# Five small moves in an attention-then-experts kernel: buffers, weight fetches, decay rows, PSUM banks, token products

## The chip, the cores and the metric

The kernel runs on one core of one Trainium2 chip. The metric is the device time of one execution in microseconds (us), here the median over several runs. The engines are TensorE (PE, with its weight loads shown apart as PEld), VectorE (DVE), ScalarE (ACT), GpSimd (POOL) and SyncE (SP, which only issues DMAs here). All data is float32, but for the one-hot rows of the token lists, which are float16.

## The reference

```python
# attention: q, k, v, alpha are (B=4, H=8, S=768, D=48); alpha lies in 0.8 to 1.0
for t in range(S):
    state = alpha[:, :, t, :, None] * state + einsum('bhd,bhe->bhde', k[:, :, t], v[:, :, t])
    y[:, :, t] = einsum('bhd,bhde->bhe', q[:, :, t], state)

# experts: x is y with its heads side by side, (N=3072, Dm=384); E=8 experts, F=1024
logits = x @ w_gate
expert = argmax(logits, axis=1)
gate_w = softmax(logits) at expert
out[n] = gate_w[n] * (relu(x[n] @ w1[expert[n]]) @ w2[expert[n]])
```

Each token goes to one expert only, and every token is kept, whatever the load of its expert.

## The kernel before

**Order.** The program is written under a manual schedule: each engine executes its instructions in the order in which the Python code emits them, and waits by semaphores for what an instruction needs. There is no planner. So a call that moves in the code moves on every engine, and a DMA stands in the queue of the engine that issues it: loads, row copies and weights on SP, the decay rows on ACT, gathers and scatters on POOL. The DMAs of SP and ACT share eight semaphores in a ring, so each of them also waits for the one eight issues earlier.

**Attention.** The sequence is cut into 6 chunks of 128 time steps. With 4 batches this makes 24 tiles; tile `s` is chunk `s // 4` of batch `s % 4`. The loop `for i in range(-4, NT)` runs one step per tile (about 5.45 us in the middle) and works on several tiles at once:

- `loads_for` fetches q, k, v and alpha, mostly for two tiles together (384 KB a load), some steps ahead.
- `logs` (L387) takes ln of alpha on ACT into `lna`; `cums` sums it over time on PE (L392, tile `cum`) and takes `icp` = exp(-sum) and `cp` = exp(sum) on ACT (L395, L396).
- `decay_out` copies the first row of `icp` of a tile, for the tile's own chunk, and the last row of `cp`, for the next chunk, into a small tile `dec` with one DMA each on the ACT queue (L408). With a chunk's first batch it also loads one row of alpha, `alpha0`, on SP (L411).
- `decay_rows` (L416, L417, POOL) multiplies these to `er`, the decay from one chunk to the next; `decay_cols` turns `er` on PE (`ep`, L428) and copies it to `E` (L430). `scale_state` (L475, POOL) makes `U`, the state times `E`.
- `operands` (L437, POOL) makes `kqb`, k times `icp` and q times `cp`, for tile `i + 2`; `transposes` (L447) turns it, with DVE copying `qT` (L451) and ACT `kT` (L453) out of PSUM.
- `scores` (L460, `sA` and `sB`), `mask` (L468, `dA` and `dB`), `read_state` (L487, reads `U`), `attend` (L497) and `keys_values` (L508) make the output of a tile in PSUM (`y`); ACT copies it to `yT` (L516). `rows` (L534) turns it into token rows `x`, and with them come the logits.
- `logits`, `gate` (L548, `gex`) and `gate_weight` choose the expert and its weight; `keep_rows` writes the weighted token row from `x` to `xs` (L559, ACT) and copies it to `x_rows` in DRAM by a DMA of 192 KB on SP (L560). The tile `xs` has the pool's default of two buffers.
- `fetch_part` fetches expert 0's weights in ten pieces (six of w1 with 256 KB, four of w2 with 384 KB), one per step from i=4 to i=13. `late_consts` makes constants of the routing on POOL, in five portions at i=1 to i=5.

In the first steps (i = -4 to 2) more than one tile is summed per step: `new_sums(i)` gives two tiles at i=1 and i=2 (tiles 4, 5 and 6, 7, chunk 1), and one afterwards.

**Between the two halves.** Expert 0's first 256 tokens are gathered before attention has ended. `early_layer1(f)` (L626) computes the block f of 8 of their hidden layer. `tokens` (L298) multiplies the one-hot rows of the last 8 tiles into the token lists `tok`; `place_experts` (L306 to L324) orders the experts by load; `weights(1, 1)` fetches the next expert's weights on SP; `decode` (L333 to L347) reads `tok` and gives in its first four operations (`ag`, `au`, `agi`) the indices of the gathers, and after that those of the scatters.

**Experts.** The experts are worked off in eight places, the largest group first after expert 0. Place 0 is the rest of expert 0's tokens (168 rows): `gather`, `early_layer2` (L1083, the second layer of the early 256 tokens), `rest_layer1` (L1095, 8 blocks into PSUM banks, the relus in turn on ACT, L1103, and DVE, L1100, with pieces of the DVE work `beside` in between) and `rest_layer2` (L1111, three blocks `d`, copied to `zT` at L1114). Places 1 to 7 use a scheme with seven products instead of eight (L875, L933, L948). PSUM has the tags `tp`, `pA`, `pB` and `pC` with two banks each. `scatter` copies a block of rows out of PSUM (`zo`, L965, ACT) and writes it to the tokens' places in `out` with an indirect DMA on POOL (L966); the rows of the last place come from `rows_layer2` (L992).

Of the kernel before, what the change touches and what calls it, by code (L numbers as in the profile page):

```python
# [8 lines left out]
F32 = mybir.dt.float32  # L9
# [9 lines left out]
def kernel(  # L19
# [343 lines left out]
    with tc.tile_pool(name="ld", bufs=6) as ld, \  # L363
# [32 lines left out]
            nc.scalar.activation(cp[:], cum[:, :Dm], AF.Exp)  # L396
            st[s]["cp"], st[s]["icp"] = cp, icp

        def decay_out(s):
            c, b = cb(s)  # L400
            cp, icp = st[s]["cp"], st[s]["icp"]


            for cc, i, row in ((c, 1, icp[0:1, :]), (c + 1, 0, cp[C - 1 :, :])):
                if 0 < cc < NB:
                    if cc not in decay:
                        decay[cc] = work.tile([B, 2, Dm], F32, name="dec", bufs=3)
                    nc.scalar.dma_start(decay[cc][b : b + 1, i, :], row)  # L408
            if b == 0 and c + 1 < NB:
                alpha0[c + 1] = work.tile([B, H, D], F32, name="alpha0", bufs=3)  # L410
                nc.sync.dma_start(alpha0[c + 1][:], alpha[:, :, (c + 1) * C, :])  # L411

# [142 lines left out]
        def keep_rows(s):  # L555

            d = st[s]
            xs = work.tile([C, NP, D2], F32, name="xs")
            nc.scalar.activation(xs[:], d["x"][:, :, :D2], AF.Copy, scale=d["gw"][:])  # L559
            nc.sync.dma_start(x_d[s * C : (s + 1) * C, :], xs[:].rearrange("p m d -> p (m d)"))  # L560
            st[s] = {n: t_ for n, t_ in d.items() if n == "acc"}
# [106 lines left out]
        for i in range(-4, NT):  # L668
            loads_for(i)
            do(scores, i)  # L670
            if i < NT - 1:
                do(result, i - 1)
            do(logits, i - 2)
            if i >= B:
                do(add_state, i - 1)
            do(gate, i - 2)
            if i > 0:
                for s in new_sums(i):
                    logs(s)
            if i == NT - 1:  # L680
                early_turn()
            if 0 < i < NT and i % B == 0:
                decay_cols(i // B)
            do(mask, i, 0)
            do(mask, i, 1)
            if i < B:
                do(add_state, i - 1)
            do(transposes, i + 1)
            sums = list(new_sums(i))
            for s in sums[:1]:  # L690
                cums(s)
            if i < 0:
                for s in sums[1:]:
                    cums(s, "x")
            do(gate_weight, i - 2)
            route(i)
            do(keep_rows, i - 2)
            if i < 0 or len(sums) == 1:
                for s in sums:
                    decay_out(s)  # L700
            if i == NT - 2:
                si = next(se)[1]
                eg["si"] = lambda j, r: si[:r, j : j + 1]
            do(operands, i + 2)
            if i % B == 0:
                do(scale_state, i)
            if 0 < i + 1 < NT and (i + 1) % B == 0:
                decay_rows((i + 1) // B)
            elif i >= 0:
                do(scale_state, i + 1)  # L710
            one_hots(nc.gpsimd, *on_gpsimd.get(i, ()))
            do(read_state, i)
            do(attend, i)
            if i == NT - 2:
                result(i)
            if i >= 0 and sums[1:]:
                cums(sums[1])
                for s in sums:
                    decay_out(s)
            do(keys_values, i)  # L720
            if i == NT - 3:
                held["tok"] = ps.tile([C, NC], F32, name="tok", tag="cum")
                tokens(held["tok"][:], *range((NG - 1) * TG))
                se = early_gather()
            do(rows, i - 1)
            if i in counts_in:
                counts(counts_in[i], counted(i - 1))
            if i < 0:
                for s in new_sums(i + 1):
                    logs(s)  # L730
            if i == -3:
                second_consts()
            late_consts(i - 1)
            if 4 <= i < 14:
                fetch_part(groups[0], i - 4)


        last = NT - 1
# [16 lines left out]
        keep_rows(last)  # L755
        slots(NG - 1, cps)
        rows_cols(NG - 1)
        for f in range(3, FB):
            early_layer1(f)
        for s in range((NG - 1) * TG, NT):  # L760
            one_hots(nc.vector, s)
            tokens(held["tok"][:], s)
        place_experts()
        weights(1, 1)
        d = decode(held["tok"][:], NC, "a")
        g_e = next(d)
        _, s_e, gf_e, sf_e = next(d)


# [190 lines left out]

        return p1, rest

    def scatter(g, j, r, zp):
        zo = wk.tile([C, Dm], F32, name="zo", bufs=3)
        nc.scalar.copy(zo[:r], zp)  # L965
        ins = nc.gpsimd.indirect_dma_start(  # L966
            out=out[:, :], out_offset=bass.IndirectOffsetOnAxis(ap=g["si"](j, r), axis=0),
            in_=zo[:r], in_offset=None, bounds_check=N - 1, oob_is_err=False,
# [119 lines left out]
    def rest_layer1(g, beside):  # L1088
        n = g["n"]
        g["h"] = wk.tile([C, FB, CAP0], F32, name="h_sb")  # L1090
        for f in range(FB):
            t = "pB" if f % 2 else "pC"
            hp = mps.tile([C, 512], F32, name=t, tag=t)
            for a in range(DB):
                nc.tensor.matmul(  # L1095
# [44 lines left out]
    for i, g in enumerate(groups):  # L1140
# [39 lines left out]
        if last:  # L1180
            for j, r in blocks(g):
                rows_layer2(g, j, (*([] if j == 0 else ready), FH - 1, FB - 1))
                scatter(g, j, r, g["z"][:r, :Dm])
        elif i:
            rest[0](lambda: ahead(*((1,) if i == E - 2 else (1, 2))), between)
        else:
# [59 lines left out]
```

## Time and profile before

| | |
|---|---|
| runs, us | 432.89, 425.61, 425.33, 430.03, 426.73, 426.06 |
| median, us | 426.4 |
| profiled execution, us | 426.63 |
| its span (first to last instruction), us | 424.8 |
| mean granted clock of TensorE | 0.993 |
| PE busy, us | 405.5 (95% of the span) |
| DVE, ACT, POOL busy, us | 207.8, 171.1, 143.8 |
| DMA moved | 59.08 MB, 139 GB/s on average |

The span is from the first to the last instruction of the profiled execution; the execution's own time is 1.8 us longer. Times of instructions are counted from the start of the span. In a row of the timeline the first number is the start, the second the duration, then come engine, line, operation, tiles and shapes; a bracket at the end gives the idle time of the engine before the row, and what ended it. "SPq" and "ACTq" rows are a queue issuing DMAs. A granted clock of 1.00 is full speed, and 0.50 is half.

### The profile page before, as it was taken

To read this page: it belongs to the slowest core of one execution; us is meant where nothing else is said; L and a number is where in the kernel's file an instruction comes from. 1 tells how busy PE (TensorE), PEld (TensorE's weight loads), DVE (VectorE), ACT (ScalarE), POOL (GpSimd) and SP (SyncE) were. 2 spreads that over 40 slices of the span, in tenths; PEclk is the share of its full clock that TensorE was granted. 3 is DMA by queue.
4 is the path that set the end of the run, shared out by engine and by line. 5 is a ranking of instruction groups with operands and counts; after the bars stand their busy time and mean duration, and the time that the engine had idled before them with its cause. 6 is when DMAs were issued, how large, how long until landed. Compare 5 with 4: busy or idle time off the path is not lost.

```text
span 424.8 us, 9224 instructions
## 1 busy us (share of the span) xinstructions
PE 405.5 (95%) x3525; PEld 342.1 (81%) x3525; DVE 207.8 (49%) x643; ACT 171.1 (40%) x453; POOL 143.8 (34%) x193
## 2 busy tenths in 40 slices
PE   7988999997999999889999999999999999999995
PEld 4757888886888885789879979979979979979952
DVE  5442555563565665174663563473473483453200
ACT  4564566564665430114413513513523523513510
POOL 3438464678558203602300340240240240200101
PEclk9998999999999999999999999999999999999998
DMA  9999999899851217644235054252351352300101
GB/s 172 189 201 209 224 242 205 210 233 233 184 124 39 96 39 253 225 149 169 75 137 169 37 210 128 78 207 74 132 205 60 144 203 58 145 1 2 51 20 35
DMA packets 120098, 59.08 MB, mean 139 GB/s; under 512 B 102934, under 2 KB 114287, under 8 KB 120052
## 3 DMA queue, kind: packets, MB, share of 16 engines
q1 hardware_dynamic: 114932, 48.80, 43.7%
q0 software_dynamic: 3424, 9.59, 6.4%
q8 instruction: 29, 0.48, 0.5%
q10 hardware_dynamic: 1696, 0.08, 0.3%
q14 instruction: 17, 0.14, 0.1%
HBM read 48.95 MB, written 9.58 MB: 138 GB/s over the span
## 4 chain that ended last, share of the span: by engine, by line
PE 82%; issue 6%; DMA 5%; DVE 3%; ACT 2%; POOL 1%; ACTq 0%; POOLq 0%; SPq 0%
PE pA L875 10%; PE pB L875 8%; PE pC L948 8%; PE pA L933 7%; PE y L497 5%; PE sA L460 5%; PE tp L447 5%; PE pB L933 4%; PE pC L875 4%; PE x L534 4%; PE cum L392 4%; PE y L487 3%; PE pC L933 2%; PE tp L791 2%; PE tp L626 2%
## 5 line engine op out<-in xcount | busy, mean ns | idle before, releaser
L966 POOL DMA_INDIRECT out_dram<-zo,sp x25 | 27.0, 1079 | 169.6 <-ACT zo L965 118.9
L184 DVE TENSOR_TENSOR h_sb<-pB,u 128x208 f32<-128x208 f32 (+6 forms) x56 | 20.1, 359 | 60.9 <-PE pB L875 43.1
L819 ACT COPY u<-pA 128x208 f32<-128x208 f32 (+6 forms) x68 | 21.6, 317 | 54.0 <-PE pA L933 50.3
L437 POOL TENSOR_TENSOR kqb<-k_sb,icp 128x384 f32<-128x384 f32 x23 | 22.9, 998 | 43.9 <-PE y L508 16.6
L948 PE MATMUL pC<-h_sb,w 128*128 128x416 f32 (+5 forms) x96 | 32.9, 496 | 0.0
L875 PE MATMUL pA<-t,s 128*128 128x208 f32 (+6 forms) x112 | 28.6, 337 | 0.6
L460 PE MATMUL sA<-qT,kT 48*128 48x128 f32 x192 | 28.0, 286 | 0.9 <-DVE qT L451 0.9
L781 POOL DMA_INDIRECT xg<-x_rows,gp x25 | 25.9, 1034 | 7.6 <-issue 6.1
L460 PE MATMUL sB<-qT,kT 48*128 48x128 f32 x192 | 28.0, 286 | 0.0
L948 PEld LDWEIGHTS pC<-h_sb,w 128*128 128x128 f32 x96 | 18.1, 190 | 12.0 <-issue 4.4
L875 PE MATMUL pA<-xgT,w 128*128 128x208 f32 (+6 forms) x112 | 27.7, 329 | 0.0
L460 PEld LDWEIGHTS sA<-qT,kT 48*128 48x128 f32 x192 | 23.4, 189 | 3.9 <-ACT kT L453 1.1
L541 DVE TENSOR_REDUCE lgn<-x 128x8 f32<-128x32 f32 x23 | 4.4, 191 | 45.3 <-PE x L534 40.3
L447 PE MATMUL tp<-ident,kqb 128*128 128x128 f32 x192 | 25.9, 278 | 0.6 <-DVE kqb L437 0.6
L534 PE MATMUL x<-iw,yT 128*64 128x104 f32 x368 | 21.6, 261 | 2.4 <-ACT xs L559 2.3
L875 PE MATMUL pB<-t,w 128*128 128x208 f32 (+6 forms) x112 | 23.4, 331 | 0.2 <-DVE h_sb L184 0.2
L447 PEld LDWEIGHTS tp<-ident,kqb 128*128 128x128 f32 x192 | 20.8, 140 | 3.4 <-issue 1.2
L460 PEld LDWEIGHTS sB<-qT,kT 48*128 48x128 f32 x192 | 23.4, 189 | 0.0
L437 POOL TENSOR_TENSOR kqb<-q_sb,cp 128x384 f32<-128x384 f32 x23 | 22.9, 998 | 0.6 <-DMA q_sb<-in_q_dram 0.3
L875 PE MATMUL pC<-xgT,w 128*128 128x208 f32 (+6 forms) x112 | 23.1, 329 | 0.0
L888 ACT ACTIVATE h_sb<-h_sb 128x416 f32<-128x416 f32 (+6 forms) x28 | 14.8, 530 | 20.5 <-DVE h_sb L184 20.1
L468 DVE TENSOR_TENSOR dA<-sA,cmask 128x512 f32<-128x512 f32 x24 | 16.5, 689 | 12.2 <-PE sB L460 12.2
(245 smaller groups left out, 957.0 us busy)
## 6 DMA issues: line engine op xcount, KB each, us to landing
w<-in_moe_w_dram SPq DMA_DIRECT2D x14, 1536.0 KB, 7.2
x_rows<-xs SPq DMA_DIRECT2D x24, 192.0 KB, 3.2
v_sb<-in_v_dram SPq DMA_DIRECT2D x10, 384.0 KB, 6.3
k_sb<-in_k_dram SPq DMA_DIRECT2D x9, 384.0 KB, 6.6
q_sb<-in_q_dram SPq DMA_DIRECT2D x9, 384.0 KB, 5.3
a_sb<-in_alpha_dram SPq DMA_DIRECT2D x8, 384.0 KB, 4.7
a_sb<-in_alpha_dram SPq DMA_DIRECT2D x8, 192.0 KB, 3.9
w<-in_moe_w_dram SPq DMA_DIRECT2D x6, 256.0 KB, 4.3
```

Source lines behind the costliest of these rows:

```text
L184: eng.tensor_tensor(out, a, b, op=ALU.add)
L437: eng.tensor_tensor(by_half(kq[:, i]), d[n].rearrange("s (a p) d -> s a p d", a=2), d[e][:].rearrange("s (a p d) -> s a p d", a=2, p=NP), ...
L447: nc.tensor.transpose(tp[:, p, :], pair(kqb[s % 3][:, i], p), ident[:])
L460: nc.tensor.matmul(t[:, p, :], lhsT=d["kT"][r : r + D, p, :], rhs=d["qT"][r : r + D, p, :], start=True, stop=True,)
L497: nc.tensor.matmul(yv(g)[o : o + D, j, :], lhsT=d["v"][:, g * NP + p, :], rhs=d["d" + "AB"[g]][:, p, :], start=(s < B and j == 0), stop=Tr ...
L534: nc.tensor.matmul(d["x"][o : o + HC, m, : D2 + E], lhsT=d["yT"][:, m // 2, m % 2, o : o + HC], rhs=iw[:, m, :], start=True, stop=True,)
L781: nc.gpsimd.indirect_dma_start(out=g["xg"][:r, j, :], out_offset=None, in_=x_d[:, :], in_offset=bass.IndirectOffsetOnAxis(ap=g["gi"](j, r) ...
L819: nc.scalar.copy(t[:, :m], bank["A"][:, :m])
L875: nc.tensor.matmul(out, lhsT=ops[n_][0], rhs=ops[n_][1], start=first and n_ == names[0], stop=True, skip_group_check=True,)
L933: nc.tensor.matmul(out, lhsT=lhs, rhs=rhs, start=first and f == 0, stop=True, skip_group_check=True)
L948: nc.tensor.matmul(d2[:, :n], lhsT=w2[:, f, 2 * C :], rhs=h[:, f, :n], start=(f == 0), stop=(f == FB - 1),)
L966: ins = nc.gpsimd.indirect_dma_start(out=out[:, :], out_offset=bass.IndirectOffsetOnAxis(ap=g["si"](j, r), axis=0), in_=zo[:r], in_offset= ...
```

## The change

- The tile `xs` gets four buffers instead of two. The ten pieces of expert 0's weights are fetched at i=12 to 21 instead of i=4 to 13.
- `decay_out` takes an argument that says which of its two rows to copy. For chunk 1, steps i=1 and i=2 copy only the `icp` rows, two DMAs instead of four; the `cp` rows of tiles 4 to 7 follow at i=3 to 6, one in each step, next to the two DMAs that these steps have already. `alpha0` of chunk 2 goes with the first of them. The rows of tiles 0 and 1 are copied at i=-1. `late_consts` is called at i=-4 (three portions), 0 and 1.
- `rest_layer1` takes its PSUM banks in turn from `pC`, `pB` and `pA` instead of `pC` and `pB`.
- The last token products come before the last block of `early_layer1` instead of after it, and the first part of `decode` comes before `place_experts`.
- The last scatter's rows (112 of them) are copied half by DVE and half by ACT, out of the same bank.

```diff
--- before.py
+++ after.py
@@ -396,17 +396,18 @@
             nc.scalar.activation(cp[:], cum[:, :Dm], AF.Exp)
             st[s]["cp"], st[s]["icp"] = cp, icp
 
-        def decay_out(s):
+        def decay_out(s, which=(0, 1)):
             c, b = cb(s)
             cp, icp = st[s]["cp"], st[s]["icp"]
 
 
-            for cc, i, row in ((c, 1, icp[0:1, :]), (c + 1, 0, cp[C - 1 :, :])):
+            for j in which:
+                cc, row = ((c, icp[0:1, :]), (c + 1, cp[C - 1 :, :]))[j]
                 if 0 < cc < NB:
                     if cc not in decay:
                         decay[cc] = work.tile([B, 2, Dm], F32, name="dec", bufs=3)
-                    nc.scalar.dma_start(decay[cc][b : b + 1, i, :], row)
-            if b == 0 and c + 1 < NB:
+                    nc.scalar.dma_start(decay[cc][b : b + 1, 1 - j, :], row)
+            if b == 0 and c + 1 < NB and 1 in which:
                 alpha0[c + 1] = work.tile([B, H, D], F32, name="alpha0", bufs=3)
                 nc.sync.dma_start(alpha0[c + 1][:], alpha[:, :, (c + 1) * C, :])
 
@@ -555,7 +556,7 @@
         def keep_rows(s):
 
             d = st[s]
-            xs = work.tile([C, NP, D2], F32, name="xs")
+            xs = work.tile([C, NP, D2], F32, name="xs", bufs=4)
             nc.scalar.activation(xs[:], d["x"][:, :, :D2], AF.Copy, scale=d["gw"][:])
             nc.sync.dma_start(x_d[s * C : (s + 1) * C, :], xs[:].rearrange("p m d -> p (m d)"))
             st[s] = {n: t_ for n, t_ in d.items() if n == "acc"}
@@ -695,9 +696,14 @@
             do(gate_weight, i - 2)
             route(i)
             do(keep_rows, i - 2)
-            if i < 0 or len(sums) == 1:
-                for s in sums:
+            if len(sums) == 1:
+                decay_out(sums[0])
+            if i == -1:
+                for s in range(2):
                     decay_out(s)
+
+            if B - 1 <= i < 2 * B - 1:
+                decay_out(i + 1, (1,))
             if i == NT - 2:
                 si = next(se)[1]
                 eg["si"] = lambda j, r: si[:r, j : j + 1]
@@ -716,7 +722,7 @@
             if i >= 0 and sums[1:]:
                 cums(sums[1])
                 for s in sums:
-                    decay_out(s)
+                    decay_out(s, (0,) if i else (0, 1))
             do(keys_values, i)
             if i == NT - 3:
                 held["tok"] = ps.tile([C, NC], F32, name="tok", tag="cum")
@@ -730,9 +736,11 @@
                     logs(s)
             if i == -3:
                 second_consts()
-            late_consts(i - 1)
-            if 4 <= i < 14:
-                fetch_part(groups[0], i - 4)
+            if i in (-4, 0, 1):
+                for j in {-4: (0, 1, 2), 0: (3,), 1: (4,)}[i]:
+                    late_consts(j)
+            if 12 <= i < 22:
+                fetch_part(groups[0], i - 12)
 
 
         last = NT - 1
@@ -755,15 +763,16 @@
         keep_rows(last)
         slots(NG - 1, cps)
         rows_cols(NG - 1)
-        for f in range(3, FB):
+        for f in range(3, FB - 1):
             early_layer1(f)
         for s in range((NG - 1) * TG, NT):
             one_hots(nc.vector, s)
             tokens(held["tok"][:], s)
+        early_layer1(FB - 1)
+        d = decode(held["tok"][:], NC, "a")
+        g_e = next(d)
         place_experts()
         weights(1, 1)
-        d = decode(held["tok"][:], NC, "a")
-        g_e = next(d)
         _, s_e, gf_e, sf_e = next(d)
 
 
@@ -960,9 +969,13 @@
 
         return p1, rest
 
-    def scatter(g, j, r, zp):
+    def scatter(g, j, r, zp, shared=False):
         zo = wk.tile([C, Dm], F32, name="zo", bufs=3)
-        nc.scalar.copy(zo[:r], zp)
+        if shared:
+            nc.vector.tensor_copy(zo[:r, : Dm // 2], zp[:, : Dm // 2])
+            nc.scalar.copy(zo[:r, Dm // 2 :], zp[:, Dm // 2 :])
+        else:
+            nc.scalar.copy(zo[:r], zp)
         ins = nc.gpsimd.indirect_dma_start(
             out=out[:, :], out_offset=bass.IndirectOffsetOnAxis(ap=g["si"](j, r), axis=0),
             in_=zo[:r], in_offset=None, bounds_check=N - 1, oob_is_err=False,
@@ -1089,7 +1102,7 @@
         n = g["n"]
         g["h"] = wk.tile([C, FB, CAP0], F32, name="h_sb")
         for f in range(FB):
-            t = "pB" if f % 2 else "pC"
+            t = "p" + "CBA"[f % 3]
             hp = mps.tile([C, 512], F32, name=t, tag=t)
             for a in range(DB):
                 nc.tensor.matmul(
@@ -1180,7 +1193,7 @@
         if last:
             for j, r in blocks(g):
                 rows_layer2(g, j, (*([] if j == 0 else ready), FH - 1, FB - 1))
-                scatter(g, j, r, g["z"][:r, :Dm])
+                scatter(g, j, r, g["z"][:r, :Dm], shared=j == NJ - 2)
         elif i:
             rest[0](lambda: ahead(*((1,) if i == E - 2 else (1, 2))), between)
         else:
```

## The prediction

> **What bounds the kernel now.** I read the page first, then PE's gaps in the timeline, then the engine that each gap names.
>
> ```profile
> PE 405.5 (95%) x3525; PEld 342.1 (81%) x3525; DVE 207.8 (49%) x643; ACT 171.1 (40%) x453; POOL 143.8 (34%) x193
> ...
> DMA  9999999899851217644235054252351352300101
> ```
>
> PE is busy 405.5 of 424.8 us, and the change takes no matmul away. So it can win only from PE's 19.3 us of idle, or from PE's clock. The second line says that DMA is full for the first ten slices (106 us) and has room afterwards.
>
> The timeline of PE; the bracket is PE's idle before the row and what ended it:
>
> ```profile
> 23.15 0.91 PE L392 MATMUL cum<-lna,cum_m 128*128 128x384 f32 x2 [0.64 <-ACT lna L387]
> ...
> 30.33 0.91 PE L392 MATMUL cum<-lna,cum_m 128*128 128x384 f32 x2 [1.05 <-ACT lna L387]
> ...
> 38.58 0.66 PE L487 MATMUL y<-qT,U 48*48 48x128 f32 x16 [1.71 <-POOL U L475]
> ...
> 105.83 0.93 PE L534 MATMUL x<-iw,yT 128*64 128x104 f32 x16 [2.33 <-ACT xs L559]
> ...
> 160.86 7.98 PE L1083 MATMUL pA<-w,h 128*128 128x384 f32 x24 [0.68 <-DVE au L334]
> 169.70 0.38 PE L791 MATMUL tp<-ident,xg 40*128 40x40 f32 x3 [0.33 <-DMA xg<-x_rows,agi]
> ...
> 179.07 1.12 PE L1095 MATMUL pC<-xgT,w 128*128 128x168 f32 x6 [1.09 <-issue]
> 181.93 1.12 PE L1095 MATMUL pB<-xgT,w 128*128 128x168 f32 x6 [1.73 <-DVE h_sb L1100]
> ```
>
> These eight gaps make 9.6 us, and each part of the change aims at some of them. The gap at 38.58 has a sequel; in the windows view the granted clock is the third number from the end:
>
> ```profile
> 34.00:39.00 5.00, 3.29 (x44) 2.53 (x42) 2.56 (x8) 2.73 (x7) 4.46 (x15) 1.00 1.18 247
> 39.00:44.00 5.00, 5.00 (x76) 4.46 (x66) 0.63 (x3) 1.39 (x4) 4.03 (x13) 0.66 1.00 195
> ```
>
> The clock was halved (0.66 on average) right after that gap. From L487 to the next tile's first score PE took 4.00 us where other steps take 2.68, and the first scores 0.27 more: about 1.6 us. After the 2.33 us gap at 103.5 the clock stayed at 1.00.
>
> **Part B, decay rows spread and constants early.** ACT issues the row copies between its own work. In the timeline of ACT (ACTq rows are issues):
>
> ```profile
> 26.14 0.55 ACTq L408 DMA_DIRECT2D dec<-icp  x1
> 26.79 0.55 ACTq L408 DMA_DIRECT2D dec<-cp  x1
> ...
> 28.07 0.55 ACTq L408 DMA_DIRECT2D dec<-cp  x1
> 28.99 0.58 ACT L516 COPY yT<-y 128x512 f32<-128x512 f32 x1 [2.08 <-PE tp L447]
> ```
>
> The issues are 0.64 us apart; taking two of the four out moves yT, and lna three operations behind it, 2 x 0.64 = 1.28 us forward. Step i=1 has the same four. The gaps at 23.15 (0.64) and 30.33 (1.05) both end on lna and are smaller than 1.28, so both close: PE reaches L487 at 36.87 - 1.69 = 35.18. What it waits for there is on POOL:
>
> ```profile
> 32.32 0.99 POOL L416 TENSOR_TENSOR er<-dec 4x384 f32<-4x384 f32 x1 [3.78 <-DMA dec<-icp]
> ...
> 35.78 1.00 POOL L437 TENSOR_TENSOR kqb<-k_sb,icp 128x384 f32<-128x384 f32 x1
> 37.06 1.00 POOL L437 TENSOR_TENSOR kqb<-q_sb,cp 128x384 f32<-128x384 f32 x1 [0.28 <-DMA q_sb<-in_q_dram]
> 38.02 0.98 POOL L475 TENSOR_TENSOR U<-acc,E 128x192 f32<-128x192 f32 x2
> ```
>
> Between er and kqb stand er's second product and nine constant operations, 34.34 to 35.82, 1.5 us; they leave (to POOL's idle at 2.24 to 7.69 and 14.47 to 17.47, which holds them). The last dec copy that er needs is issued some 1.9 us sooner (second place instead of fourth, ACT ahead by the first gap), so er and both kqb could run about 3 us sooner. But the second kqb needs q_sb, landed at 36.93, and PE started 1.65 us after that landing. Ends: q_sb lands as now, L487 stays at 38.58, gain 0 (the 1.69 us only move into this wait); or it lands by 33.5, U is no longer late, gain 1.69 + 1.71 = 3.4. Its issue at 32.06 waited on a dec copy's semaphore and stood behind a k issue of 3.26 us. Both shrink with fewer copies in the queue, while DMA remains full. I take a landing at 35.0: start 36.65, gain 1.9. The half clock goes with a shorter gap (36.65 - 35.18 = 1.5 against 1.71), which is far from sure; I take 1.0 of its 1.6 us. B: -2.9, from 0 to -5.0. Were the gap to grow to 3.4, a second half-clock stretch of 1.6 would be the loss.
>
> B also adds: at i=3 to 6 a third copy per step, 0.64 us before yT, against some 0.23 us of slack there, so yT is 0.4 late. I cost this at nothing, since gex behind it waits for lmin anyway and PE reads yT one step later; without that cover it is 4 x 0.4 = 1.6 us. Chunk 2's er waits for a copy issued 1.2 us later (55.5 to 56.7); its transposes come only near 60. alpha0's small load moves from i=1 to i=3 on SP, past no one who waits for it.
>
> [...]
>
> **Part A, four xs tiles and later weights.** With two tiles, xs waits for the x_rows copy of two tiles before:
>
> ```profile
> 105.20 0.58 ACT L559 ACTIVATE xs<-x,gw 128x384 f32<-128x384 f32 x1 [2.68 <-DMA x_rows<-xs]
> ```
>
> With four this copy has two more steps, 10.9 us, to land; the whole 2.33 us of PE at 105.83 goes. x_rows had been issued at 99.75 and took 5.36 us, beside loads and a weight part (issued 101.38). The ten weight issues now come at i=12 to 21, each on SP behind that step's loads and x_rows. They sit beside loads for about six steps instead of ten, then beside an almost idle DMA. Next late could be the loads: 1.92 MB of loads and row copies per two steps (10.9 us) at some 200 GB/s is 9.6 us, which leaves 1.3 for two weight parts, 0.5 to 0.75 MB. So I keep an end of -1.0; taken -2.3, the other end -2.4. The last is issued in step 21, near 131 (step 4 at 38.6, 5.45 us each), and lands well before PE needs it at 160.86.
>
> **Part D, three bank pairs.** In place 0 each layer-1 block takes 0.855 us of PE, and PE stopped before f=6 (179.07) and f=7 (181.93). Four banks made f=4 and f=5 wait for the relus of f=0, 1, harmless, and f=6, 7 for those of f=2, 3. With six, f=6, 7 need only f=0, 1. But those relus were late without cause on their engines:
>
> ```profile
> DVE h_sb L1100 <- PE pB L1095: 5.1, 1, 5.1
> DVE h_sb L1100 <- PE pC L1095: 5.0, 1, 5.0
> ACT h_sb L1103 <- PE pB L1095: 4.7, 1, 4.7
> ```
>
> The view of waits (total, times, longest) shows each waiting 5 us for a PE block that by PE's own rows ended 3 to 5 us earlier. No bank explains that. If the signals stay late, DVE still gets f=3 at 181.54 and runs the planner's work between its relus (f=5 183.34, f=7 184.91), and layer 2 ends at 185.84 as before: gain 0. If they come in time, f=7 ends at 179.5 and layer 2's first block near 182: gain 3.8. I take 1.2, nearer to the row.
>
> **Part E, token products sooner.** The 0.68 us at 160.86 waited for decode's second operation, which waits for the token products at 159.82. The one-hots were done at 158.35, so the products can stand before the last early block (158.53, 1.3 us), which then covers decode: the gap closes, unless something else is late. gi is ready some 1.3 us sooner, so the gather should close 0.33 at 169.70 too. place_experts' eight operations are pushed behind decode's four (0.85 us), and the SP weight fetches behind them by 1.7; their first reader is DVE at 185.16, with room. Ends -0.2 and -1.0; taken -0.7.
>
> **Part F, the last copy split.**
>
> ```profile
> 419.80 0.48 ACT L965 COPY zo<-pB 112x384 f32<-112x384 f32 x1 [4.73 <-PE pB L992]
> ```
>
> As built, ACT's half carries a wait on DVE, DVE's on PE: the halves run one after the other. 192 columns are 0.35 on DVE (L524 copies as many out of PSUM) and 0.30 on ACT (its 208-column rows are 0.32), the handover some 0.08: 0.73 instead of 0.48. Side by side it would be 0.35. Ends -0.13 and +0.35; taken +0.2.
>
> [...]
>
> **Sum.** -2.9 - 2.3 - 1.2 - 0.7 + 0.2 = -6.9 against the profiled run's 426.6 us (span 424.8 and 1.8 around it), the median of the runs being 426.4: 419.7.
>
> **The rivals.**
> (1) The waits only move: q_sb lands as now (B 0), the signals stay late (D 0), A -1.5, E -0.5, F +0.2: -1.8, 424.8. For it: DMA is full up to 106 us, and no part moves fewer load bytes before 80 us except the weights. Against it: the gaps name ACT's copies and xs, not loads.
> (2) Everything opens: -2.4 - 5.0 - 3.8 - 1.0 = -12.2, with F 0: 414.4. For it: no loss on the path but F; against it: D's late signals.
> (3) Slower: late weights on SP, ahead of the next steps' k and q at i=12 to 17, where DMA is still full. They push the landings past kqb's lead of two steps, so that PE waits in every one of six steps, as once at 105.83. At 2.33 us each that is +14.0, and with the other parts (-2.9 - 1.2 - 0.7 + 0.2 = -4.6) it gives 436.0. It decides from about 1.5 us per step upward (4.1 to the bound of slower, and 4.6, over six). Against it: before, the same parts lay at i=4 to 13 with full DMA, and PE hardly waited.
>
> **How the numbers follow.** Forecast 419.7 (its own range 416 to 423) 0.60; rival 1, 0.22; rival 2, 0.10; rival 3, 0.08. About 1% (4.3 us) can be told from no change here: faster is below 422.1, slower above 430.7. Faster: 0.52 of the forecast, all of rival 2, and 0.08 for rival 1's better half: 0.70; same 0.22; slower 0.08. The range 415.0 to 425.2 leaves out half of rival 2, rival 3 and a part of rival 1: 2 in 10.
>
> **What would show it.** B right: no idle before cum at 23 and 30, U's end below 37.3, granted clock 1.00 between 36 and 44. A right: no idle near x at 104, and kqb never waits on k_sb or q_sb. D right: f=6 and f=7 back to back; undecided if layer 2 still ends on DVE's relus. E: no idle before L1083. F: ACT's half starts at DVE's end. The prediction is wrong if PE waits for loads after 80 us, or if PE's idle total falls by less than 4 us.

## The result and the profile after

The changed kernel takes 423.57 us (median of 33 runs, 420.10 to 425.87), the kernel before 426.32 us (median of 70 runs, 421.78 to 432.89). The ratio is 0.9958, with a 95% interval of 0.9943 to 0.9973: faster, by 0.4%, where 1.6% had been predicted. The ratio leaves out the executions that took over 1.5% more than the fastest of their kernel (some 20 of the 70 before, none of the 33 after), so it shows less gain than the two medians. The profiled execution took 424.30 us, with a span of 422.6. The time lies in the range of the prediction, but the gain is a quarter of what was forecast.

Where the profile gives each part's gain can be read by taking PE's matmuls in order (both kernels have 3525) and subtracting the start of each in the profile before from its start in the profile after:

| PE has reached (time before, us) | difference, us |
|---|---|
| 20.8, first steps | -0.27 |
| 32.3, after the two gaps before L392 | -1.63 |
| 39.8, after L487 | -1.15 |
| 43.0, after the stretch at half clock in before | -2.62 |
| 51.2, after a new gap at 48 | -2.09 |
| 102.6, before the wait for xs | -1.92 |
| 106.7, behind it | -4.45 |
| 174.7, in place 0's first layer | -5.22 |
| 183.5, start of place 0's second layer | -8.58 |
| 189.7, end of place 0 | -2.44 |
| 417.9, end | -2.44 |

So 5.2 us were won before place 0, 3.4 in its first layer, and 6.1 were lost in its second. The timeline of PE after the change (the bracket is the idle time before the row):

```profile
28.70 0.91 PE L392 MATMUL cum<-lna,cum_m 128*128 128x384 f32 x2 [0.58 <-ACT lna L387]
...
37.43 0.66 PE L488 MATMUL y<-qT,U 48*48 48x128 f32 x16 [2.15 <-POOL U L476]
...
48.13 0.91 PE L392 MATMUL cum<-lna,cum_m 128*128 128x384 f32 x2 [0.39 <-ACT lna L387]
...
156.22 4.14 PE L1096 MATMUL pA<-w,h 128*128 128x384 f32 x12 [0.47 <-ACT h L631]
...
176.53 1.30 PE L1124 MATMUL pA<-h_sb,w 128*128 128x168 f32 x4 [1.20 <-issue]
178.31 0.84 PE L1124 MATMUL pA<-h_sb,w 128*128 128x168 f32 x4 [0.48 <-DVE h_sb L1113]
179.89 0.93 PE L1124 MATMUL pA<-h_sb,w 128*128 128x168 f32 x2 [0.75 <-DVE h_sb L1113]
```

The wait for xs is gone; the one for U has grown from 1.71 to 2.15; the two of place 0 have moved from layer 1 to layer 2. What comes of them there is seen in the windows (PE's busy time is the first number behind the comma, the granted clock third from the end):

```profile
174.00:177.00 3.00, 1.80 (x12) 1.37 (x10) 0.82 (x5) 0.08 (x1) 0.89 (x1) 1.00 0.30 81
177.00:180.00 3.00, 1.63 (x8) 0.99 (x7) 2.83 (x13) 0.43 (x2) 0.00 (x0) 0.86 0.32 57
180.00:182.00 2.00, 2.00 (x9) 1.95 (x10) 1.97 (x4) 0.30 (x1) 0.00 (x0) 0.50 1.03 422
...
184.00:186.00 2.00, 2.00 (x9) 2.00 (x8) 0.00 (x0) 0.00 (x0) 0.00 (x0) 0.50 0.00 0
```

PE is busy for 3.4 of the 6 us from 174 to 180, and then works at half clock until 186. The waits of 2.4 us and the half clock (half of 6 us, and 14% of 1.6 busy us before it: 3.2) make 5.6 of the 6.1. Why the relu of block f=3 is late is not told by PE's rows. PE's row of that block, and DVE's relus, of which f=3's came after 5.33 us of idle:

```profile
170.04 1.02 PE L1108 MATMUL pC<-xgT,w 128*128 128x168 f32 x6
```

```profile
169.38 0.33 DVE L1113 TENSOR_SCALAR h_sb<-pB 128x168 f32<-128x168 f32 x1 [4.18 <-PE pB L1108]
...
176.14 0.33 DVE L1113 TENSOR_SCALAR h_sb<-pC 128x168 f32<-128x168 f32 x1 [5.33 <-PE pA L1124]
177.94 0.31 DVE L1113 TENSOR_SCALAR h_sb<-pA 128x168 f32<-128x168 f32 x1
179.51 0.33 DVE L1113 TENSOR_SCALAR h_sb<-pB 128x168 f32<-128x168 f32 x1
```

DVE's rows are f=1, 3, 5, 7. PE's block f=3 ended at 171.06, and its signal reached DVE at 176.1.

### The profile page after: what moved, and what is told of

Same layout as the page of the kernel before. It is cut to its first block, busy times and chain, and to the rows that moved or that the text cites. A ratio compares the mean times of both kernels' runs of the same rounds, so it can differ in the third digit from the quotient of the medians.

```text
span 422.6 us, 9225 instructions
## 1 busy us (share of the span) xinstructions
PE 406.6 (96%) x3525; PEld 343.3 (81%) x3525; DVE 208.6 (49%) x644; ACT 170.7 (40%) x453; POOL 144.0 (34%) x193
## 4 chain that ended last, share of the span: by engine, by line
PE 83%; issue 6%; DMA 4%; DVE 2%; ACT 2%; POOL 2%; ACTq 0%; SPq 0%; POOLq 0%
PE pA L884 10%; PE pB L884 8%; PE pC L957 8%; PE pA L942 7%; PE sA L461 5%; PE tp L448 5%; PE y L498 5%; PE pB L942 4%; PE pC L884 4%; PE x L535 3%; PE cum L392 3%; PE pA L1096 3%; PE y L488 2%; PE pC L942 2%; PE pA L1124 2%
## 5 line engine op out<-in xcount | busy, mean ns | idle before, releaser
L448 PEld LDWEIGHTS tp<-ident,kqb 128*128 128x128 f32 x192 | 20.8, 140 | 3.4 <-issue 1.2
L517 ACT COPY yT<-y 128x512 f32<-128x512 f32 x24 | 14.1, 586 | 19.4 <-PE y L509 10.1
```

The costliest lines, as they stand in the source:

```text
L448: nc.tensor.transpose(tp[:, p, :], pair(kqb[s % 3][:, i], p), ident[:])
```

## The experiments

The kernels were run in five series (the expectations say "call" for a series). The kernels of a series share runs of the kernel before; ratios are to those, with a 95% interval. Its median was 420.3 us in the first series and 421.0 in the last, but 425.4, 425.7 and 426.0 in the three between, so times are compared within a series only. "Late" means below that PE's signal of a finished block in place 0 reached ACT or DVE 2 to 6 us after the block's end. T1, T2 and so on are the names that the expectations give to their theories.

### First series: the bank pairs and their neighbours

Place 0 of the changed kernel with two bank pairs:

```diff
-            t = "p" + "CBA"[f % 3]
+            t = "pB" if f % 2 else "pC"
```

> The changed kernel with place 0's banks as before (pC and pB only). Theory T1 (three pairs let PE run ahead, so that its waiting comes together in 174 to 180 us, and the clock is halved from about 180 to 186): no half clock in place 0, PE's waits there again 1.1 and 1.7 us before f=6 and f=7, time near 421 us, 2 to 3 us below the changed kernel. Theory T2 (the half clock of place 0 is chance and has nothing to do with the banks; the missing gain was never there in the other parts): about 423.5 as the changed kernel, and half clock in place 0 or elsewhere as often.

Measured: 417.32 us, ratio 0.9925 (0.9894 to 0.9956).

The kernel before with the three pairs alone (the same line the other way):

> The kernel before with only the three bank pairs. T1: PE waits for nothing before f=6 and f=7, then about 2.5 us within 6 us before layer 2's products, half clock for about 6 us after it; net 2 to 3 us slower than before. T2: equal to before, or up to 2 us faster.

Measured: 419.74, ratio 0.9996 (0.9964 to 1.0027). With no relu late in either profile (below), neither of these two runs decides between T1 and T2.

DVE's planning work behind the relus:

```diff
                 nc.vector.tensor_scalar_max(g["h"][:, f, :n], hp[:, :n], 0.0)
-                next(beside, None)
...
+        for _ in beside:
+            pass
```

> The changed kernel, with DVE's planning work of place 0 put behind the four relus on DVE instead of between them. T1: f=5 and f=7 are relu'd right after f=3, so the waits of 0.48 and 0.75 us in layer 2 go; the wait for f=3's late signal (1.2 us) stays. With less waiting in one window the clock stays at 1.00 and the time is near 418.5, 5 us below the changed kernel. If the half clock comes anyway after the one wait of 1.2 us or more: about 422.5. T2: as the changed kernel.

Measured: 420.12, ratio 0.9999 (0.9967 to 1.0032), 2.8 us worse than the first kernel. The planning work now stands before DVE's copy of xgT, and PE waits 1.98 us for that.

The second group's gathers behind place 0's second layer:

```diff
-        if i + 2 < E:
+        if i and i + 2 < E:
             gather(groups[i + 2])
...
             rest_layer2(g, 2)
+            gather(groups[2])
```

> The changed kernel, with the second of the two groups of four gathers that POOL starts during place 0 (the one for the group of place 2) put behind place 0's second layer. Theory G (PE's signals reach the other engines late because of the gathers in flight): the relus of f=2 and f=3 start within 0.1 us of their blocks' ends, PE waits under 0.3 us in place 0, clock 1.00, time near 418. Rival theory S (the lateness lies in this stretch of PE's own program): relus of f=2 and f=3 still 2 to 5 us late, time as the changed kernel.

Measured: 417.44, ratio 0.9926 (0.9896 to 0.9955). The edit moved nothing: POOL has no other instruction between the old place and the new, and the gathers start at the same point (from 170.49 in its profile, as from 170.21 before the edit). This kernel is the changed kernel once more, and theory G is not tested.

None of the four profiles has a late relu, with two pairs or three. In DVE's timeline of the one with two pairs, f=3's row starts after 0.28 us of idle, at its block's end:

```profile
168.66 0.33 DVE L1113 TENSOR_SCALAR h_sb<-pB 128x168 f32<-128x168 f32 x1 [4.18 <-PE pB L1108]
170.37 0.33 DVE L1113 TENSOR_SCALAR h_sb<-pB 128x168 f32<-128x168 f32 x1 [0.28 <-PE pB L1108]
```

PE then has no wait over 0.3 us in place 0. So where the signals are in time, the pairs are worth nothing, and the rest of the change is worth 2.9 us (0.7%; the changed kernel itself, 2.8).

### Second series: the change again, and two parts alone

> The changed kernel unaltered. Theory P (PE's late signals in place 0 belong to some executions or to one chip, not to the kernel; where they are absent the bank pairs are worth nothing, and the rest of the change is worth about 3 us): if place 0's relus of f=2 and f=3 start at once, the time is 2.5 to 3.5 us below before on the same chip; if they start 2 to 5 us late, a half clock follows in place 0 and the gain is 0 to 3 us. Theory K (the changed kernel always has the half clock in place 0): late relus and half clock here too, gain below 3 us, about 6 us above the same kernel with two pairs.

Measured: 423.93, ratio 0.9964 (0.9939 to 0.9989). The relus are late again (f=3 starts at 177.51 after 6.03 us of idle DVE), and PE waits 2.8 us in layer 2.

> The kernel before unaltered, for its profile beside the others of this call. P: place 0 shows the same lateness, or its absence, as in the changed kernel's profile of this call; the waits for xs and U may differ from the first profile. K: place 0 waits 1.1 and 1.7 us as in the first profile.

One execution: 425.41 us. Place 0 is late here too (2.45 us before f=7), and half clock follows in it. The other waits differ from the first profile: 0.56 us for U and no half clock after it, and 0.87 and 1.10 us for xs at 57 and 81 us in place of one wait of 2.33.

Four xs tiles and the later weights, on the kernel before:

```diff
-            xs = work.tile([C, NP, D2], F32, name="xs")
+            xs = work.tile([C, NP, D2], F32, name="xs", bufs=4)
...
-            if 4 <= i < 14:
-                fetch_part(groups[0], i - 4)
+            if 12 <= i < 22:
+                fetch_part(groups[0], i - 12)
```

> The kernel before with four xs tiles and the weight pieces at i=12 to 21. From the first profile: no wait for xs, 2.3 us below before. If such a wait is not in every execution (0.3 and 0.5 us in the run with the bank pairs alone): 0.5 to 1.5 us below.

Measured: 423.52, ratio 0.9966 (0.9929 to 1.0003), so 1.4 us of gain, between 3.0 and nothing. Its profile has no wait for xs over 0.2 us.

The decay rows and constants, on the kernel before (the three pieces of the diff that concern `decay_out` and `late_consts`):

> The kernel before with only the decay rows spread and the constants early. From the prediction: 2.9 us below before; from the changed kernel's trace, where this part took 2.7 and a third issue on ACT gave 0.8 back: 1.9 below. Rival: U waits for the loads however it is, 0 to 1 below.

Measured: 426.03, ratio 0.9999 (0.9964 to 1.0035), as the rival said (0 to 1 below). PE's timeline in its one profile:

```profile
36.61 0.66 PE L488 MATMUL y<-qT,U 48*48 48x128 f32 x16 [2.02 <-POOL U L476]
...
56.47 0.94 PE L535 MATMUL x<-iw,yT 128*64 128x104 f32 x16 [0.99 <-ACT xs L560]
81.11 0.94 PE L535 MATMUL x<-iw,yT 128*64 128x104 f32 x16 [1.61 <-ACT xs L560]
105.15 0.93 PE L535 MATMUL x<-iw,yT 128*64 128x104 f32 x16 [1.62 <-ACT xs L560]
```

The two gaps before L392 are gone. PE gets to U sooner and waits longer; 0.8 us of gain is left at that point (36.61 against 37.41 in the profile of before in this series), and the waits for xs, 4.53 us against 1.97, take more than the rest. That is one execution of each; the timed runs say only that the part alone gives 0, with 1.5 us either way.

### Third series: the same questions where the signals are late

> The changed kernel with place 0's banks as before. Theory T1 (where PE's signals of place 0 come late, three pairs gather PE's waiting in 5 us and the clock halves after it): if the relus of f=2 and f=3 are late here, PE waits before f=6 and f=7 instead, with no or a shorter half clock, and the time is 4 to 6 us below before, against 1.5 to 2.8 for the changed kernel on such a chip. Rival T2 (two pairs wait as long and the clock halves as well): 1.5 to 2.8 below before. Without late relus: 3 below, and nothing told apart.

> The changed kernel with the second group of gathers behind place 0's second layer. Theory G (signals are late while the eight gathers are in flight): on a chip whose other profiles show late relus, here f=2 and f=3 are relu'd in time or nearly, no half clock in place 0, 6 to 8 us below before. Theory S (the lateness belongs to this stretch of PE's program, or to the first four gathers and the weight loads): relus late as in the others, 1.5 to 3 below.

> The kernel before with the three bank pairs alone. T1: with late relus, half clock in place 0 and 0.5 to 3 us above before. T2: 0 to 2 below before. Without late relus: no difference.

Two pairs: 423.52, ratio 0.9967 (0.9934 to 1.0000). Three pairs (the second kernel, again the changed kernel itself, as its gathers stay where they were): 423.37, ratio 0.9965 (0.9931 to 1.0000). Three pairs on the kernel before: 427.24, ratio 1.0036 (0.9996 to 1.0077). All three profiles have late relus. In PE's timeline of the kernel with two pairs there is one long wait:

```profile
176.02 2.05 PE L1108 MATMUL pB<-xgT,w 128*128 128x168 f32 x6 [3.17 <-DVE h_sb L1113]
```

with three it waits in pieces, in layer 2: 2.0 us in the changed kernel, 3.2 in the kernel before with three pairs. The executions of the two changed kernels have mean clocks of 0.991 and 0.989 (medians). For the changed kernel T2 holds: two pairs and three take the same time, 423.52 and 423.37. On the kernel before, the 1.5 us above it (0.2 below to 3.3 above) lie where T1 had put them and not T2, so a small loss by the pairs is not excluded. But two pairs do not keep the clock up, as T1 needs: among the profiles with late relus, half clock stands in place 0 in five of six with two pairs and in four of five with three.

> The changed kernel with two bank pairs, the second group of gathers behind place 0, and the last copy whole on ACT: the best version that the traces suggest. G: 6 to 8 us below before where signals are late, 3 where they are not, and the last scatter starts 0.24 us sooner after PE's last product than in the changed kernel. S: as the two pairs alone.

Two pairs and the last copy whole on ACT: 422.22, ratio 0.9931 (0.9900 to 0.9962). Its gather edit moved nothing either, so it differs from the first kernel of this series by the last copy only, which the traces put at 0.24 us. The 1.3 us between the two are not explained by it, and the intervals overlap.

### Fourth series: what holds U, and what holds the signals

k and q of tiles 6 and 7 first:

```diff
-            if i > 1:
+            if i == 2:
+                for n in "akqva":
+                    load_next(n, 2)
+            elif i > 1:
```

> The changed kernel, with the loads of step i=2 in another order: k and q of tiles 6, 7 ahead of v of tiles 4, 5 and of alpha of tiles 10, 11. Theory L (U waits for k_sb and q_sb, whose landing at 34 to 36 us is set by the loads ahead of them; so the decay rows' part only lengthened PE's wait): both kqb of tile 6 follow er at once, U is done near 34.5, PE's wait of 1.7 to 2.1 us before L488 falls below 0.5 us, the time is 1.5 to 2 us below the changed kernel, unless v or alpha stalls the next step by as much. Rival (POOL's own work or er's rows set U): PE's wait stays above 1.5 us and the time stays.

Measured: 419.33, ratio 0.9865 (0.9807 to 0.9923). On POOL, after and then with this edit:

```profile
30.77 1.00 POOL L418 TENSOR_TENSOR er<-er,alpha 4x384 f32<-4x384 f32 x1
34.48 1.00 POOL L438 TENSOR_TENSOR kqb<-k_sb,icp 128x384 f32<-128x384 f32 x1 [2.70 <-DMA k_sb<-in_k_dram]
35.92 0.99 POOL L438 TENSOR_TENSOR kqb<-q_sb,cp 128x384 f32<-128x384 f32 x1 [0.44 <-ACT icp L395]
36.87 0.99 POOL L476 TENSOR_TENSOR U<-acc,E 128x192 f32<-128x192 f32 x2
```

```profile
31.37 0.99 POOL L418 TENSOR_TENSOR er<-er,alpha 4x384 f32<-4x384 f32 x1
32.34 0.99 POOL L438 TENSOR_TENSOR kqb<-k_sb,icp 128x384 f32<-128x384 f32 x1
33.29 1.00 POOL L438 TENSOR_TENSOR kqb<-q_sb,cp 128x384 f32<-128x384 f32 x1
34.26 0.98 POOL L476 TENSOR_TENSOR U<-acc,E 128x192 f32<-128x192 f32 x2
```

In the changed kernel POOL is ready at 31.8, waits 2.70 us for k_sb, and then 0.44 us more: q_sb, issued at 30.49, took 5.29 us and landed at 35.78, just before the second kqb (the row names ACT). With k and q first POOL goes straight through, PE's wait at L488 is 0.21 us, and its start there (34.81) is 2.6 us sooner than in the first profile of the changed kernel. Theory L holds. In time the edit did more than that: by the ratios, 0.9865 against 0.9958, some 4 us, but the changed kernel was not run in this series, and there are six runs.

Four of the eight gathers really moved, behind the scatters of place 0's rows:

```diff
-        if i + 2 < E:
-            gather(groups[i + 2])
+        if i == 1:
+            gather(groups[2])
+        if 0 < i < E - 2:
+            gather(groups[i + 2])
```

> The changed kernel, with the second group's gathers held back on POOL behind the scatters of place 0's rows, so that they run in place 1 (about 195 us); the earlier attempt left them in place 0, since nothing stood before them on POOL. Theory G (signals are late while these gathers are in flight): on a chip with late relus, the relus of f=2 and f=3 now come within 0.1 us of their blocks' ends, PE does not wait in place 0, the clock stays at 1.00 there, time 4 to 6 us below the changed kernel; if late signals then show in place 1, a part of it comes back. Theory S (the lateness belongs to this stretch of PE's program or to what went before): f=2 and f=3 late by 2 to 5 us as in all runs on such chips, time unchanged. On a chip without late relus nothing is told apart.

Measured: 420.88, ratio 0.9891 (0.9843 to 0.9938). In the run before this one, in the same series, f=3's relu was late (5.25 us of idle DVE before it); here is DVE's row of f=3 in the timeline:

```profile
171.32 0.33 DVE L1113 TENSOR_SCALAR h_sb<-pC 128x168 f32<-128x168 f32 x1 [0.37 <-PE pC L1108]
```

and, in PE's timeline, a wait in place 1:

```profile
205.30 1.06 PE L942 MATMUL pC<-h_sb,w 128*128 128x208 f32 x2 [2.67 <-ACT h_sb L897]
```

The lateness has left place 0, but for 0.9 us at f=2, and shows up in place 1, where this kernel now issues eight gathers in a row (192.7 to 202.6), with half clock from 204.7 to 211.5 behind the wait. That speaks for theory G and against S: the lateness went where the gathers went. The gain is smaller than the 4 to 6 us of G, as a part came back in place 1. No other profile has a wait in that spot, but the next one, which has the same eight:

> The changed kernel with both edits, two bank pairs and the last copy whole on ACT. If L and G hold: 6 to 8 us below the changed kernel where signals are late, 1.5 to 2 where not. If only L: 1.5 to 2. If neither: 0 to 1.

Measured: 418.21, ratio 0.9832 (0.9787 to 0.9878); place 0 free of waits, 2.67 us of wait in place 1.

### Fifth series: never eight gathers in a row

```diff
-        if i + 2 < E:
-            gather(groups[i + 2])
+        if 0 < i < E - 1:
+            gather(groups[i + 1])
```

> The changed kernel with k and q first in step i=2, each place gathering for the next place only (four gathers per place, behind that place's scatters, so never eight in a row), and the last copy whole on ACT. G and L: no late relus in place 0 and no wait of 2.7 us in place 1, PE without a wait over 0.5 us from 10 to 400 us, clock 1.00 but at the ends; 9 to 12 us below before where signals were late, 5 to 6 where not. Rival: a gather that starts one place later lands too late for its rows' turn, and PE waits up to a few us per place.

Measured: 414.80 us, ratio 0.9872 (0.9823 to 0.9920), the lowest time on record (by its ratio the last kernel of the fourth series, 0.9832, is as good). PE's timeline has one wait over 0.35 us between 10 us and the end:

```profile
153.22 7.04 PE L1099 MATMUL pA<-w,h 128*128 128x384 f32 x21 [0.47 <-ACT h L634]
```

and the mean clock is 0.999. The later gathers cost PE no wait here. The gain, 5.4 us by the ratio, is the 5 to 6 that were expected where signals are in time, and by two marks they are in this series: before takes 421.0, and the profiles have as many DMA landings recorded (3353) as those of the first series (3352 or 3353), where all with late signals have 3114 to 3140. So this series does not show what four gathers per place do to late signals.

> The kernel before, with none of the change, but with the two edits (k and q first, gathers for the next place only). If the two edits carry most: place 0 free of waits (about 4 us below before where signals are late), the waits for U, lna, xs and decode remain: 3 to 6 below before, 3 to 5 above the same edits on the changed kernel. Rival: loads first gives nothing without the decay rows spread, since er comes late (32 us): then U near 36, and 2 to 4 below before.

Measured: 420.57, ratio 0.9994 (0.9956 to 1.0032). Without the change the loads' order gives nothing, for the rival's reason, though not with its numbers (U near 36, 2 to 4 us below before): er's first product starts at 31.7, the constants still stand behind it, and U's first half is done at 37.6; the waits for lna, xs (1.82 and 1.83 us) and decode are all there. No relu is late in place 0. The changed kernel with the same edits, and the last copy whole, is 5.8 us faster (420.57 - 414.80): with k and q first the change is worth about twice the 2.9 us of the first series, where signals were in time as well.

> The first kernel of this call with two bank pairs instead of three. Without late signals the banks are no limit: equal within 0.5 us. If three pairs still matter: 1 us or more above it.

Measured: 415.26, ratio 0.9875 (0.9830 to 0.9920): with signals in time, two pairs and three are equal within the measurement.

## Why the prediction was right or wrong

**The base of the sum.** Each gap of one profiled execution was taken as the kernel's. The gaps before L392 (0.6 and 1.0, the second also 1.8 and 2.1) and before L1083 (0.7 to 0.8) came back in every profile that has these places as before. The wait for U did not: in the five profiles with the decay rows and loads of before (the kernel before twice, the three pairs alone twice, tiles and weights alone) it was 1.71, 0.56, 1.27, 0 and 0.34 us, so the first profile had the longest, and only there did half clock follow. In the first 106 us, where DMA is full (172 to 242 GB/s in the ten slices of before's page), a wait for a DMA moves from run to run by as much as the gains claimed.

**A, -2.3.** In the pair of profiles it brought 2.53 (from -1.92 to -4.45 in the table). In the six profiles with two xs tiles PE's waits for xs sum to 2.33, 1.97, 2.18, 0.81, 3.65 and 4.53 us, 2.6 on average, and in none of the profiles with four tiles is there one over 0.2. Timed alone the part is worth 1.4 us (0 to 3.0), which includes 2.3. The mechanism held, the size is not contradicted, and PE waited for no load after 50 us, so the late weights disturbed nothing. One sign that was set for it failed on account of B: kqb was never to wait on k_sb or q_sb, and waited 2.70 us.

**B, -2.9.** This is the step that failed, and it failed in the two terms that were taken from the first profile's wait for U. That the two gaps before L392 close came as worked out (-1.36 in the table, by 32 us; 0.58 of the second stays in that profile, as lna waits there for alpha's load). So did the start at L488: in the ten profiles that have this part with the loads in their old order, q_sb landed at 34.7 to 35.8, on average at 35.2 where the prediction took 35.0; its kqb started 0.13 to 0.14 us later every time, and PE started at 36.3 to 37.4, on average at 36.8 (36.65). k_sb, to which the prediction gave no wait, held POOL for 0.6 to 2.7 us, but q_sb always landed behind it. What was mis-sized is the gain against before. PE's start there, 38.58, was the latest of the five profiles named above, whose average is 38.0, so the start brings 1.2 us (1.15 in the pair) and not 1.9. And the half clock's 1.0 was no gain. The prediction tied it to a shorter wait; but PE came to U 2.3 us sooner on average and waited 1.7 to 2.2 us there, 1.9 on average, where it had been 0.8, and half clock followed in four of the ten profiles, against one of the five. That it went away in the pair of profiles was luck. Timed alone the part gives 0 (1.5 us either way). With this part in place, k and q first bring 2.0 us more at L488 (34.85 on average in four profiles): the price of the part was the landing of the loads.

What goes with half clock is seen in the times of the clock's changes, better than in the length of a gap (1.71 us with half clock behind it in before, 2.15 without in after). In each of the twenty traces they lie whole multiples of 3.41 us apart (before: 5.63, 39.76, 43.18, 422.06; after: 5.08, 179.16, 185.98, 421.50), on a grid of such stretches. Up to PE's last matmul, all 11 stretches at full clock in which PE was busy for less than 48% were followed by half clock, 6 of the 18 between 49% and 59%, and none of the others. The stretch at the wait for U, and the next one, in before; then the same in after:

```profile
36.35:39.76 3.41, 1.70 (x30) 0.99 (x29) 1.23 (x4) 1.40 (x4) 3.01 (x9) 1.00 1.20 246
39.76:43.18 3.42, 3.42 (x48) 3.17 (x46) 0.46 (x3) 0.66 (x2) 2.58 (x7) 0.50 0.87 166
```

```profile
35.80:39.21 3.41, 1.78 (x46) 1.59 (x48) 0.19 (x2) 0.92 (x3) 1.94 (x3) 1.00 1.18 231
```

In before the whole wait fell into one stretch, and PE was busy for 50% of it; in after the grid cut the wait in two (35.28 to 35.80 and on to 37.43), which left 52%. Both shares lie in the zone where either came. So in these traces the busy share of a stretch of the grid goes with what follows, not the length of one gap, and this pair lay at the border; the grid's place against the kernel's start differs from run to run (the first change comes at 4.45 to 7.68 us).

The third copy per step on ACT was costed at nothing, with 0.4 us a step as the price without cover. One step paid in this profile (and one, 0.51 us at 47, in that of the two pairs in the third series); in ACT's timeline after the change (x2: two issues in one row):

```profile
44.18 2.57 ACTq L409 DMA_DIRECT2D dec<-cp  x2
46.79 0.59 ACT L517 COPY yT<-y 128x512 f32<-128x512 f32 x1 [2.40 <-PE sB L461]
```

Two issues took 2.57 us there instead of 1.1. The cover named was lmin's wait; lna stands behind yT as well, was late, and PE waited 0.39 us at 48.13 (the table loses 0.5 there). The second of the two issues took 1.97 us; an issue was priced by its usual duration of 0.55, and why this one took longer the rows do not tell.

**D, -1.2.** This term was mis-sized too. The lower end was right and the value was not: 0 in the changed kernel, with late signals and without. The reading that "no bank explains that" was right, and should have ended in 0, though one of the three rows shown with it is f=1's relu, which came only 0.5 us behind its block; late were those from f=2 on. Missing from the bounds was a loss: the half clock in place 0, which nine of the eleven profiles with late signals show, and which took 3.2 us in the profiled execution. The kernel before is the one profile with late signals and two pairs that has no half clock there, so the 6.1 us that the table loses are in part luck of the pair.

**E, -0.7.** No run has this part alone. Between 106.7 and 174.7 us the table gives 0.77, of which 0.6 falls between 161 and 170, at the gather. The waits for decode and for the gather went, and a new one of 0.47 for the relu of the last early block came, which now ends closer to its reader.

**F, +0.2.** The timeline of all engines near the end, after the change:

```profile
417.32 0.36 DVE L975 COPY zo<-pB 112x192 f32<-112x192 f32 x1 [11.87 <-PE pB L1005]
417.75 0.32 ACT L976 COPY zo<-pB 112x192 f32<-112x192 f32 x1 [5.12 <-DVE zo L975]
```

The halves go one after the other, as the prediction said, 0.43 us apart, and the last scatter starts 0.24 us later after PE's last matmul than before.

**The rivals.** What happened is nearest to the first: the waits only moved, for U and in place 0. Its 424.8 is 1.2 us above what was measured. It had been given 0.22, against 0.60 for the forecast. With what the runs show, A at -1.4 as timed, B at 0 (timed alone) to -1.2 (at U), D at 0, E at -0.7 and F at +0.2, the sum is -1.9 to -3.1; the ratio says -1.8 (1.2 to 2.4 us), the medians -2.75. The prediction's own sign against it came too: PE's idle time fell by 3.3 us, from 19.3 to 16.0, where less than 4 was to mean that it is wrong.

## What to carry to other kernels

Before a gap is booked as a gain, ask for the second releaser: the engine that ends the wait may itself have a DMA that lands just behind the work being removed, and that is then the price. A gap in a stretch where DMA is full varied from run to run here (the wait for U from 0 to 1.71 us, those for xs from 0.81 to 4.53 in sum), so a sum needs the gaps of two or three profiles, not one; and a half clock behind such a gap is not a gain to be counted on, as long as the gap stays (it came in one of five profiles without part B, and in four of the ten with it). When a stall has no cause on the engines it names, as in place 0, more buffers on those engines may only move it, as the third bank pair did here (423.52 us with two pairs, 423.37 with three): look for what else is in flight, and move that.

## What the runs showed of the hardware

- With eight gathers in a row on POOL (most of 128 rows, 1.3 us apart, in place 0 two sets of four with one scatter between), PE's completion signals reached ACT and DVE up to 5.8 us late, several together: in the changed kernel's trace signals arrive at 172.56 and 176.12, and five more from 176.89 on, 0.08 us apart. With four of them moved to place 1, the lateness in place 0 fell to about 0.9 us and a wait of 2.67 us came in place 1, in both profiles with that edit. All eleven profiles of the main pair and of the second to fourth series with eight gathers in place 0 show the lateness, and none of the four of the first series, which has the same gathers. What differs between those runs stays open, and so does the mechanism. It is not the chip alone: the first and the fourth series are noted under the same chip. Where signals are late, some 210 to 240 of the 3353 DMA landings are also missing from the record; since every run's span and clock were recorded, it is open whether recording takes part in the lateness.
- The kernel before took 420.3 us in the series whose profiles had no late signals, 421.0 in the last series, whose profiles had none either, and 425.4 to 426.0 in the series where they had.
- The granted clock changed only at whole multiples of 3.41 us from one another, in all twenty traces, and half clock lasted one or two such stretches (3.41 or 6.82 us) wherever it came before the end. Executions of the changed kernel have mean clocks from 0.985 to 1.000; the one at 1.000 took 420.10 us, the least of its 33.
